# The last value chunk loaded into two spare half buffers in a two-part decode attention kernel

## The chip, the cores and the metric

The kernel runs on one core of one Trainium2 chip. The metric is the time on the device in microseconds (us), median of several executions. The record gives each execution a state; it was "fast" for every one (mean granted clock 0.93 to 0.94). Times in the traces count from the start of the span, which is 1.7 to 2.0 us shorter than the timed run.

## The reference

Two attention layers decode one token each for 4 sequences. A has 8 KV heads for 32 query heads and looks at the last 2048 keys; B has 32 heads of its own and looks at all 8192. Everything is bf16. The code is shortened.

```python
def _B_ref(x, k_cache, v_cache, wq, wo):          # A: the same on k_cache[:, :, Sk - W:, :], each KV head for 4 heads
    q = (x @ wq).reshape(B, Sq, H, Dh).transpose(0, 2, 1, 3)
    scores = jnp.einsum("bhqd,bhkd->bhqk", q, k_cache) * (Dh ** -0.5)
    p = _softmax(scores, axis=-1)
    o = jnp.einsum("bhqk,bhkd->bhqd", p, v_cache)
    return o.transpose(0, 2, 1, 3).reshape(B, Sq, H * Dh) @ wo
```

Only the caches are large: B's K and V are 268 MB each. The kernel has to stream them once.

## The kernel before

The work is cut into 72 chunks: 8 for A (c = 0 to 7, one KV head each) and 64 for B (c = 8 to 71, two heads of one sequence each, 4 MB of keys and 4 MB of values). K and V chunks go through ten half buffers of 16 KB per partition. B uses halves 0 to 3 for keys and 4 to 7 for values, two halves per chunk, in turn. Halves 8 and 9 serve A only.

```python
HALF_A = {"k": (2, 3, 8, 0, 1), "v": (6, 7, 9, 4, 5)}
LASTV = (64, 32, 16, 16)                           # the last value chunk comes in four pieces

def take(load, at, n, release):                    # a load waits for whatever last held its halves
    waits = []
    for i in range(at, at + n):
        waits += held[i]
        held[i] = [release]
    half_of[load] = at
    return waits

def dma_kv(kind, c):
    ...
    at = HALF_A[kind][c % 5] if ch["ab"] == 0 else (0 if kind == "k" else 4) + 2 * (c % 2)
    waits = take((kind, c), at, 1 if ch["ab"] == 0 else 2, ("T", ch["s_last"]) if kind == "k" else ("pv", c))
    ...
    if kind == "v" and c == NC - 1:
        j0 = 0
        for i, n in enumerate(LASTV):
            x = slice(j0 * P, (j0 + n) * P)
            sch.add_dma("sp", lambda e, x=x: e.dma_start(dst[:, x], src[:, x]), "d_vl%d" % i, waits=waits, key=("vl", j0))
            j0 += n
        return
    sch.add_dma("sp", lambda e: e.dma_start(dst, src), "d_h%d" % at, waits=waits, key=(kind, c))

loads = [("k", c + 1) for c in range(NC - 1)]      # each value chunk behind the next key chunk,
for c in range(NC):                                # but the last three at the very end
    loads.insert(2 * c + 1 if c < NC - 3 else len(loads), ("v", c))
```

(Cuts are marked with "...".) So the queue ends with k69, v68, k70, k71, v69, v70, v71. All loads go in this order through one queue. TensorE transposes a key chunk (T), makes scores (S), and multiplies weights with values (PV, 128 matmuls per chunk, "pv69" for chunk 69). In the loop the PV of one chunk is woven into the end of the next chunk's scores. At the end the order differs:

```python
for c in range(NC):
    keys_part(c)
    ...
    if c == NC - 2:
        emit_qb(c + 1)                             # no PV here
    else:
        values_part(None if c == 0 else c - 1 if c < NC - 1 else c - 2, c)
    if c == NC - 1:
        values_only(c - 1, c)                      # pv70
emit_fin(NC - 3)
emit_wos(NC - 1)
norm_sum(NC - 1)
values_only(NC - 1, NC)                            # pv71
emit_fin(NC - 1)
```

TensorE's program is a loop over pairs of chunks; chunks 70 and 71 stand behind it as straight code of 906 matmuls, each with its weight load.

## Time and profile before

| | before |
|---|---|
| time, median of the three runs given at the start | 1390.22 us (1389.66 to 1393.65) |
| span of the profiled run | 1388.5 us |
| bytes moved | 588 MB, mean 423 GB/s |
| TensorE / VectorE / ScalarE busy | 84% / 48% / 30% |
| waits of pv71 for its pieces of v71 | 5.16 us in all |

How to read it: "busy" of TensorE is an average over a kernel that waits for key chunks (150 us for B's, before the transposes), so it does not name the bound. The prediction shows the lines from which the bound is read. In these lines "tr" is T, "sc" is S, "po" is PV, "fin" is the output projection and "ms" a small sum; "issue" marks idle time in which the engine waited for nothing that the profile shows.

### The profile page before, as it was taken

How to read it: one execution, taken by the hardware profiler on the slowest of the kernel's cores; microseconds unless marked ns; L12 is line 12 of the kernel's file. 1: busy time of each engine (PE TensorE's matmuls, PEld its weight loads, DVE VectorE, ACT ScalarE, POOL GpSimd, SP SyncE). 2: the span in 40 equal slices, each digit the busy share in tenths (PEclk: the TensorE clock that was granted, in tenths of full speed). 3: DMA queues.
4: the chain of work that ended last, by engine and by line, in shares of the span. 5: the costliest groups of instructions: out<-in, count | busy, mean ns of one | idle time of the engine just before them, and what ended most of it. 6: DMA issues, size and time to landing. Idle time of an engine off the chain costs nothing.

```text
span 1388.5 us, 57015 instructions
## 1 busy us (share of the span) xinstructions
PE 1167.4 (84%) x26768; PEld 1124.6 (81%) x26768; DVE 673.0 (48%) x1327; ACT 422.9 (30%) x617; POOL 19.2 (1%) x22
## 2 busy tenths in 40 slices
PE   4778868998888888888888888988898888988887
PEld 4767868988888888888888888888888788887886
DVE  2877534554445444444445444544444444544452
ACT  1333322332233332332333232332233233332331
POOL 1111000000000000000000000000000000000000
PEclk9999989999999999999999999999999999999998
DMA  9999999999999999999999999999999999999995
GB/s 398 417 415 424 426 429 423 432 425 436 430 432 433 428 433 428 434 427 432 430 436 429 429 429 435 432 429 430 430 432 430 430 430 435 427 428 431 434 417 237
DMA packets 29992, 588.02 MB, mean 423 GB/s; under 512 B 2656, under 2 KB 10864, under 8 KB 11120
## 3 DMA queue, kind: packets, MB, share of 16 engines
q1 hardware_dynamic: 29912, 587.22, 99.0%
q8 instruction: 40, 0.66, 0.2%
q14 instruction: 16, 0.13, 0.0%
q10 hardware_dynamic: 24, 0.01, 0.0%
HBM read 587.21 MB, written 0.01 MB: 423 GB/s over the span
## 4 chain that ended last, share of the span: by engine, by line
DMA 60%; PE 33%; DVE 5%; issue 2%; ACT 0%; SPq 0%; DVEq 0%
DMA kv<-in_B_k_cache_dram 57%; PE tr L320 21%; PE sc L322 9%; DMA kv<-in_A_k_cache_dram 2%; PE po L322 2%; DVE kt L383 1%; DVE sA L432 1%; DMA kv<-in_B_v_cache_dram 1%; DVE rsa L500 1%; PE ms L322 1%; DVE sel L425 1%; DVE rm L442 0%; DVE sA L489 0%; DVE rs L498 0%; ACT eA L492 0%
## 5 line engine op out<-in xcount | busy, mean ns | idle before, releaser
L320 PE MATMUL tr<-identb,kv 128*128 128x128 bf16 x8704 | 699.7, 231 | 161.2 <-DMA kv<-in_B_k_cache_dram 150.2
L383 DVE COPY kt<-tr 128x1024 bf16<-128x1024 bf16 x736 | 502.8, 691 | 472.6 <-PE tr L320 468.6
L320 PEld LDWEIGHTS tr<-identb,kv 128*128 128x128 bf16 x8704 | 555.3, 104 | 187.6 <-issue 104.1
L381 ACT ACTIVATE kt<-tr 128x1024 bf16<-128x1024 bf16 x352 | 360.2, 1023 | 648.3 <-PE tr L320 645.7
L322 PE MATMUL sc<-qb,kt 128*128 128x64 bf16 x8192 | 422.4, 196 | 5.1 <-issue 2.9
L322 PEld LDWEIGHTS sc<-qb,kt 128*128 128x128 bf16 x8192 | 348.9, 100 | 8.7 <-issue 4.6
L322 PE MATMUL po<-pbb,kv 128*128 128x64 bf16 (+1 forms) x8192 | 290.8, 192 | 16.3 <-issue 10.9
L322 PEld LDWEIGHTS po<-pbb,kv 128*128 128x128 bf16 x8192 | 263.8, 97 | 15.8 <-issue 8.2
L481 ACT ACTIVATE pbb<-sc,negb 64x128 bf16<-64x128 f32 x128 | 51.1, 399 | 294.6 <-DVE negb L471 288.7
L447 DVE TENSOR_REDUCE rm<-sc 64x1 f32<-64x128 f32 x128 | 36.9, 289 | 94.0 <-PE sc L322 93.1
L322 PE MATMUL sc<-qs,kt 128*128 128x64 bf16 (+3 forms) x512 | 25.6, 194 | 17.0 <-DVE kt L383 17.0
L471 DVE COPY negb<-ms 128x1 f32<-128x1 f32 (+1 forms) x72 | 11.4, 158 | 52.6 <-PE ms L322 52.6
L322 PEld LDWEIGHTS sc<-qs,kt 128*128 128x128 bf16 x512 | 20.5, 99 | 20.1 <-DVE kt L383 20.0
L459 DVE TENSOR_REDUCE gm<-ms 1x2 f32<-1x128 f32 (+1 forms) x72 | 20.1, 279 | 31.3 <-PE ms L320 31.1
L322 PE MATMUL ms<-identf,gx 1*128 1x1 f32 (+1 forms) x144 | 27.2, 256 | 0.6 <-DVE gx L463 0.6
L322 PEld LDWEIGHTS ms<-identf,gx 1*128 1x128 f32 (+1 forms) x144 | 21.1, 182 | 4.9 <-DVE gx L463 0.8
L481 ACT ACTIVATION_READ_ACCUMULATOR pbb<-sc,negb 64x1 f32 x128 | 23.7, 185 | 0.0
L320 PE MATMUL ms<-identf,rm 128*1 128x128 f32 (+1 forms) x72 | 19.6, 273 | 0.2 <-DVE rm L447 0.2
L322 PE MATMUL fin<-wos,oz 128*4 128x512 bf16 x64 | 19.4, 385 | 0.3 <-DVE oz L541 0.3
L322 PE MATMUL po<-pba,kv 128*128 128x64 bf16 x512 | 18.8, 193 | 0.0
L432 DVE TENSOR_REDUCE sA<-sel 128x128 f32<-128x512 f32 x16 | 17.0, 1060 | 0.5
L463 DVE TENSOR_SCALAR gx<-gm 1x128 f32<-1x128 f32 (+1 forms) x72 | 16.0, 222 | 2.5
(46 smaller groups left out, 180.0 us busy)
## 6 DMA issues: line engine op xcount, KB each, us to landing
kv<-in_B_k_cache_dram SPq DMA_DIRECT2D x64, 4096.0 KB, 27.0
kv<-in_B_v_cache_dram SPq DMA_DIRECT2D x63, 4096.0 KB, 31.3
kv<-in_A_k_cache_dram SPq DMA_DIRECT2D x8, 2048.0 KB, 27.8
kv<-in_A_v_cache_dram SPq DMA_DIRECT2D x8, 2048.0 KB, 26.5
kv<-in_A_wq_dram SPq DMA_DIRECT2D x1, 4096.0 KB, 12.5
kv<-in_B_wq_dram SPq DMA_DIRECT2D x1, 4096.0 KB, 27.5
wor<-in_A_wo_dram SPq DMA_DIRECT2D x8, 512.0 KB, 23.4
wor<-in_B_wo_dram SPq DMA_DIRECT2D x8, 512.0 KB, 33.6
```

Source lines behind the costliest of these rows:

```text
L320: emit = lambda e: e.transpose(o, l, r)
L322: emit = lambda e: e.matmul(o, l, r, start=start, stop=stop)
L381: sch.add("act", lambda e: e.activation(dst, src, ACTF.Copy), waits=waits, key=("ev", s))
L383: sch.add("dve", lambda e: e.tensor_copy(dst, src), waits=waits, key=("ev", s))
L425: sch.add("dve", lambda e: e.tensor_tensor(out=sel[:, :].rearrange("p (j b c) -> p j b c", b=NB, c=REP), in0=sc[:, half, :].rearrange("p ( ...
L432: sch.add("dve", lambda e: e.tensor_reduce(out=dst, in_=sel[:, :].rearrange("p (j b c) -> p j c b", b=NB, c=REP), axis=AX.X, op=ALU.add), ...
L447: sch.add("dve", lambda e, src=src, pp=pp: e.tensor_reduce(out=rm[pp, m, 0:1], in_=src, axis=AX.X, op=ALU.max), waits=[("S", ch["s_last"]) ...
L459: sch.add("dve", lambda e: e.tensor_reduce(out=gm[0:C, m, 0:U], in_=src, axis=AX.X, op=ALU.max), waits=[("trm", c)], key=("gmax", c))
L463: sch.add("dve", lambda e: e.tensor_scalar(out=dst, in0=gv, scalar1=-scale, scalar2=None, op0=ALU.mult), waits=[("gmax", c)], key=("gx", c))
L471: sch.add("dve", lambda e: e.tensor_copy(negb[:, m, 0:C], ms[:, col:col + C]), waits=[("bc", c)], key=("negb", c))
L481: sch.add("act", lambda e, src=src, pp=pp, n=n, u=u: e.activation(pbv[pp, :, u], src, ACTF.Exp, bias=negb[pp, m, 0:1], scale=scale, accum_ ...
L500: sch.add("dve", lambda e: e.tensor_tensor(out=rst[0][:, m, :].rearrange("p (b c) -> p b c", b=NB), in0=bcast(rs4[:, m, :], [[0, NB], [1, ...
```

## The change

V71 has to wait for half 6 until pv69 is done, and pv69 comes late in the reordered tail. Halves 8 and 9 have been idle since chunk 7. The change puts v71 there:

```diff
             at = HALF_A[kind][c % 5] if ch["ab"] == 0 else (0 if kind == "k" else 4) + 2 * (c % 2)
+            if kind == "v" and c == NC - 1:
+                at = 8
             waits = take((kind, c), at, 1 if ch["ab"] == 0 else 2, ("T", ch["s_last"]) if kind == "k" else ("pv", c))
```

The intent is to issue v71 right behind v70, so that the stream has no hole and pv71 finds its data.

## The prediction

> **What bounds the kernel now.** I read the views from the coarse to the fine: the page, the waits of the DMA queue, the chain that ended last in its last 160 us, then the last 50 us engine by engine. The page first: the rows of the DMA busy share and of the bytes moved, in 40 slices of 34.7 us.
>
> ```profile
> DMA  9999999999999999999999999999999999999995
> GB/s 398 417 415 424 426 429 423 432 425 436 430 432 433 428 433 428 434 427 432 430 436 429 429 429 435 432 429 430 430 432 430 430 430 435 427 428 431 434 417 237
> q8 instruction: 40, 0.66, 0.2%
> ```
>
> The reader is to see a kernel that streams 588 MB at some 430 GB/s with no hole, except in the last slice: share 0.5, 237 GB/s. Nothing before the last slice can be gained by a change that moves no fewer bytes. What is left is the last 35 us. The third line counts fetches of instructions: 40 packets of 16 KB. It matters below.
>
> The waits of the DMA queue, and that queue's issues in order of time (start, duration, line):
>
> ```profile
> SPq L287 <- PE po L322: 34.5, 1, 34.5
> ...
> 1331.09 4.93 SPq L290 DMA_DIRECT2D kv<-in_B_v_cache_dram  x2
> 1370.51 1.85 SPq L287 DMA_DIRECT2D kv<-in_B_v_cache_dram  x4
> ```
>
> Line 287 is the load of the last value chunk, v71 (4 MB in four pieces). The two value chunks before it, v69 and v70, are issued at 1331.09 and 1335.69. Then the queue waits 34.5 us, once, for a PV group (out = weights times values) on TensorE. That is pv69: v71 goes to half 6, which v69 fills until pv69 ends at 1370.5. By the landings in the trace k71, v69 and v70 arrive at 1348.7, 1358.4 and 1368.1, so that the queue has run dry before v71 is issued. Busy time in stretches (length; PE, PEld, DVE, ACT, POOL; clock, DMA share, GB/s):
>
> ```profile
> 1356.00:1362.00 6.00, 4.25 (x91) 4.05 (x88) 2.82 (x7) 2.49 (x5) 0.00 (x0) 1.00 0.92 390
> 1362.00:1368.00 6.00, 5.77 (x162) 5.65 (x160) 2.82 (x6) 2.40 (x4) 0.00 (x0) 1.00 0.27 109
> 1368.00:1371.50 3.50, 3.24 (x96) 3.04 (x93) 1.06 (x5) 0.91 (x4) 0.00 (x0) 1.00 0.07 19
> 1371.50:1377.00 5.50, 4.00 (x113) 3.42 (x108) 0.52 (x2) 0.00 (x0) 0.00 (x0) 1.00 0.96 372
> ```
>
> The hole is from 1362 to 1371.5, and not sharp at its start: the completion packets of v70 lie between 1361.3 and 1367.6, so some of the 16 engines run 6 us behind others. The tail on TensorE (idle before, and its releaser, in brackets):
>
> ```profile
> 1358.51 0.29 PE L322 MATMUL sc<-qb,kt 128*128 128x64 bf16 x4 [1.75 <-issue]
> 1364.71 0.35 PE L322 MATMUL sc<-qb,kt 128*128 128x64 bf16 x6 [0.23 <-issue]
> 1370.74 3.92 PE L322 MATMUL po<-pbb,kv 128*128 128x64 bf16 x128 [0.26 <-DVE oz L541]
> 1374.59 0.59 PE L322 MATMUL fin<-wos,oz 128*4 128x512 bf16 x2
> 1375.11 0.39 PE L322 MATMUL ms<-rsb,onesf 128*128 128x4 f32 x2
> 1379.12 1.84 PE L322 MATMUL po<-pbb,kv 128*128 128x2 bf16 x64 [3.62 <-DMA kv<-in_B_v_cache_dram]
> 1381.64 1.01 PE L322 MATMUL po<-pbb,kv 128*128 128x2 bf16 x32 [0.67 <-DMA kv<-in_B_v_cache_dram]
> 1382.90 0.59 PE L322 MATMUL po<-pbb,kv 128*128 128x2 bf16 x16 [0.25 <-DMA kv<-in_B_v_cache_dram]
> 1384.11 0.58 PE L322 MATMUL po<-pbb,kv 128*128 128x2 bf16 x16 [0.62 <-DMA kv<-in_B_v_cache_dram]
> 1385.02 1.01 PE L322 MATMUL fin<-wos,oz 128*4 128x512 bf16 x2 [0.33 <-DVE oz L541]
> ```
>
> PV of chunk 70 is done at 1374.66, a last projection and a sum at 1375.5, and then TensorE waits 3.62 + 0.67 + 0.25 + 0.62 = 5.16 us for the pieces of v71. This wait is the whole of what the change can take away. After pv71 (1384.69) come 3.8 us that stay: normalisation, projection, copy, store, to 1388.5.
>
> [...] the landings 9.7 us apart agree with a stream in order. [...]the 40 packets are of 16,384 bytes; the two "issue" waits above lie exactly 256 TensorE instructions apart, the weight loads counted[...].
>
> **The change, part by part.**
>
> 1. Removed: the wait of v71 for pv69. Halves 8 and 9 were last used by key chunk 7 and value chunk 7 of the sliding part, done by about 130 us, so the new wait is over 1200 us before it is asked. v71 is issued right behind v70, at about 1336 to 1338 instead of 1370.5 to 1371.8. No instruction, byte or semaphore is added.
>
> 2. When v71 lands: the slowest engine ends v70 at 1367.6 and then has 256 KB of v71. It took 1.22 us per 32 KB: 9.8 us, so 1377.4, and about 0.5 us to the landing as with v70 (1367.6 to 1368.1): 1377.9 instead of 1384.1. The pieces: half at 1373.0, then 1375.4, 1376.7, 1377.9.
>
> 3. When TensorE could use it, if nothing else changed: from 1375.5. 128 matmuls with 2 columns, 64 in 1.84 us: 3.7 us, to 1379.2. The last 16 need the piece of 1377.9 and are reached at 1378.7, so the data is just in time. 1384.69 - 1379.2 = **5.5 us** gained at most.
>
> 4. What takes part of it back: the fetches. In the hole of before the DMA engines were free. Packet by packet: the block begun at 1358.51 has the fetch of its successor started at 1362.24, 3.7 us later; the one begun at 1364.71, in the hole, after 1.0 us; the one begun at about 1368.7 after 0.5 us; the one begun at 1373.2, with v71 flowing, after 3.4 us. From the start of a fetch to the first instruction of its block took 2.34 us (1356.17 to 1358.51) and 2.47 us (1362.24 to 1364.71) where TensorE stood waiting. So with the stream running a block of 256 can't come oftener than every 6.0 to 6.5 us, while the PV stretches use it in about 4. The straight code before the loop shows the same, again 256 instructions apart:
>
> ```profile
> 171.21 0.34 PE L322 MATMUL po<-pbb,kv 128*128 128x64 bf16 x6 [1.13 <-issue]
> 177.41 0.19 PE L322 MATMUL po<-pbb,kv 128*128 128x64 bf16 x1 [1.85 <-issue]
> ```
>
> With the change the stream has no hole. The block begun at 1364.71 is followed at 1364.71 + 6.2 to 6.5 = 1370.9 to 1371.2; TensorE gets there at 1368.7: 2.3 us lost. The next block begins near 1371.0 and TensorE is through it 4.5 us later, 1375.5; its successor arrives 2.9 us (an engine that has finished v71, as seven of them have by 1371.5) to 6.3 us (one still busy) after 1371.0, so 0 to 1.8 us are lost, 0.8 us as my middle. The one after that is asked for when most engines are free; nothing lost. Sum **3.1 us**.
>
> 5. So pv70 ends at 1374.66 + 3.1 = 1377.8, pv71 runs from 1378.6 to 1382.3, all of its data being there, and the end is 1384.69 - 1382.3 = **2.4 us** earlier.
>
> **Rivals.**
> (a) The fetches are quick enough: 5.5 us, 1384.7 us. For it: [...] the fetch in the hole may have been needed no sooner. Against: the 1.75 us at 1356.76 and the two lines above.
> (b) v71 is the new bound: a slow engine that also carries a fetch (each packet took about 1.1 us) ends v71 near 1378.5 to 1379.0, so pv71 ends at about 1379.7: 5.0 us gained if fetches don't stall TensorE, no change to point 5 if they do.
> (c) Both fetches fall on the engines that lag and stall 2.5 and 1.8 us, and a third stalls too: 5 us lost, gain near 0.5 us, 1389.7 us.
> (d) v71 in the queue early slows k71, v69 or v70: would cost up to 10 us. [...] I give it little.
> (e) It is hidden anyway: no, the 5.16 us of waits are on the chain that ended last.
>
> **Range and chances.** The timed median is 1390.22; point 5 gives 1390.2 - 2.4 = **1387.8 us**. Rival (a) at 1384.7 sets the lower side and (c) the upper; with the spread of the three runs of before (1389.66 to 1393.65) I take **1384.8 to 1390.2** for 8 in 10. 2% are 27.8 us, more than the whole stretch from the landing of v70 (1368.1) to the end of the span (20.4 us), so within 2% has **0.985**; faster 0.005, slower 0.01 for something unseen.
>
> **What the trace of after would show.** The four issues of v71 at 1336 to 1338 and no wait of 34 us on the queue; the DMA share over 0.9 from 1362 to about 1371, then falling; landings of v71 ending near 1378; no wait of the last PV for v_cache, or under 0.5 us; new "issue" waits of TensorE of 2 to 2.5 us in pv69 near 1369 and of 0 to 1.8 us in pv70 near 1375. Wrong it would be if these waits are missing (then it is faster, a), if they are longer or three (c), or if the landing of v71 slips beyond 1380.

5.5 us at most, less 3.1 us for the fetches, is the 2.4 us. A "block" in point 4 is 256 instructions of TensorE: that far apart lie the two "issue" waits that end at 1358.51 and 1364.71. Its 2.9 and 6.3 us for a fetch, and its 6.0 to 6.5 us for a block, are estimates from the times shown there: 0.5 us in the hole or 3.7 us in the stream until the fetch begins, and 2.34 to 2.47 us from there, which makes 2.8 to 6.2. That nothing can be gained before the last slice is an inference from the page (the load queue's packets fill 99.0% of the 16 engines' span; the full slices, the fourth to the 38th, carry 423 to 436 GB/s); no run tried a faster stream.

## The result

| | before | after |
|---|---|---|
| median, same rounds (4 runs each) | 1391.12 us | 1386.97 us (1385.85 to 1389.73) |
| span of the profiled run | 1388.5 us | 1384.0 us |
| v71 issued, from the span's start | 1370.5 to 1371.8 | 1339.6 to 1341.0 |
| v71 landed, last piece | 1384.06 | 1379.35 |
| pv71 | 1379.12 to 1384.69 | 1376.87 to 1380.22 |

The ratio is 0.9971 (95% interval 0.9949 to 0.9994): the mean time of one kernel's fast runs over that of the other's fast runs of the same rounds, so not quite the ratio of the medians above. It is 4.0 us, within 2%, but clear of zero. The predicted 1387.8 us lies 0.8 us from the measured median.

The page of the profile after, the same two rows of 40 slices:

```profile
DMA  9999999999999999999999999999999999999997
GB/s 398 416 416 423 425 428 421 417 428 434 430 433 430 428 431 434 429 428 432 430 434 430 429 431 433 431 427 432 429 435 429 431 430 433 431 429 430 430 409 319
```

The last slice has 319 GB/s instead of 237. What is missing to 430 now lies at its end (305 GB/s from 1371.5 to 1377, 20 from there to the last byte at 1379.35, no load after it), no longer in a hole within.

The issues of the DMA queue after (line numbers are two higher than before):

```profile
1334.60 4.93 SPq L292 DMA_DIRECT2D kv<-in_B_v_cache_dram  x2
1339.57 1.94 SPq L289 DMA_DIRECT2D kv<-in_B_v_cache_dram  x4
```

V71 follows v70 at once; the wait of 34.5 us is gone. Busy time in the stretches that the prediction shows of before:

```profile
1356.00:1362.00 6.00, 6.00 (x139) 5.92 (x136) 3.96 (x10) 3.97 (x7) 0.00 (x0) 1.00 1.01 434
1362.00:1368.00 6.00, 4.78 (x144) 4.55 (x139) 2.41 (x6) 1.02 (x1) 0.00 (x0) 1.00 0.95 404
1368.00:1371.50 3.50, 2.48 (x52) 2.26 (x53) 0.33 (x2) 0.70 (x3) 0.00 (x0) 0.80 0.94 400
1371.50:1377.00 5.50, 5.49 (x132) 4.90 (x130) 0.27 (x1) 0.21 (x2) 0.00 (x0) 0.82 0.75 305
```

The DMA share in the second and third stretch is 0.95 and 0.94, where it was 0.27 and 0.07. TensorE (first busy column) is less busy there than it was (4.78 against 5.77 us in 6; 2.48 against 3.24 in 3.5). Its timeline says why:

```profile
1366.58 0.19 PE L324 MATMUL po<-pbb,kv 128*128 128x64 bf16 x1
1368.76 1.08 PE L324 MATMUL po<-pbb,kv 128*128 128x64 bf16 x31 [1.98 <-issue]
...
1370.95 5.22 PE L324 MATMUL po<-pbb,kv 128*128 128x64 bf16 x128 [0.26 <-DVE oz L543]
1376.10 0.59 PE L324 MATMUL fin<-wos,oz 128*4 128x512 bf16 x2
1376.62 0.39 PE L324 MATMUL ms<-rsb,onesf 128*128 128x4 f32 x2
1376.87 3.35 PE L324 MATMUL po<-pbb,kv 128*128 128x2 bf16 x128
```

Three things are to be seen. Pv71 is one line of 128 matmuls and waits for nothing: the 5.16 us are gone. In pv69 TensorE stands still for 1.98 us and waits for nothing that the profile shows ("issue"). And pv70 takes 5.22 us where it took 3.92.

The trace's DMA packets settle the first of the two losses. The 256-instruction block whose first instruction comes at 1368.76 was fetched by a packet that began at 1366.25 and took 0.92 us; the block before it had begun at 1362.56. So the fetch began 3.7 us after that block, with the stream flowing, and its code ran 6.2 us after it.

The second loss has two parts. The next block boundary, at 1374.78, costs 0.20 us. The granted clock is at half from 1370.1 to 1373.5, and the starts of pv70's matmuls are 53 ns apart until 1373.45, then about 29: some 48 matmuls at 24 ns more, 1.1 us. The half clock began 1.3 us after the idle time of 1.98 us had ended and lasted 3.4 us.

### The profile page after: what moved, and what is told of

The parts are those of the page before. It is cut to its first block, busy times and chain, and to the rows that moved or that the text cites. A ratio compares the mean times of both kernels' runs of the same rounds, so it can differ in the third digit from the quotient of the medians.

```text
span 1384.0 us, 57015 instructions
## 1 busy us (share of the span) xinstructions
PE 1168.8 (84%) x26768; PEld 1125.1 (81%) x26768; DVE 672.5 (49%) x1327; ACT 422.9 (31%) x617; POOL 19.2 (1%) x22
## 4 chain that ended last, share of the span: by engine, by line
DMA 58%; PE 35%; DVE 5%; issue 2%; ACT 0%; SPq 0%; DVEq 0%
DMA kv<-in_B_k_cache_dram 55%; PE tr L322 21%; PE sc L324 9%; PE po L324 3%; DMA kv<-in_A_k_cache_dram 2%; DVE kt L385 1%; DVE sA L434 1%; DVE rsa L502 1%; PE ms L324 1%; DVE sel L427 1%; DVE rm L444 0%; DVE sA L491 0%; DVE rs L500 0%; ACT eA L494 0%; PE fin L324 0%
```

## The experiments

All kernels are edits of the changed one unless said. Calls of four runs shared the runs of the kernel before, whose medians were 1391.13, 1390.85 and 1389.52 us. The second of these calls (before_again, after_third, small16, small32) ran on another chip than the other two, so ratios are compared, not times.

**The changed kernel again, three times (after_again, after_third, after_fourth).** No edit.

> The changed kernel unaltered, for a tighter time and a second profile. Theory (the wait for v71 is gone, TensorE is the bound of the tail and stalls for instruction blocks while the stream runs): 3.5 to 5 us under the kernel before, ratio about 0.997; a stall of about 2 us in pv69, 256 instructions before a second, smaller one in pv70; no wait of pv71 for the value load. Rival (the first profile was a lucky one and the gain is the 2.4 us of the prediction): ratio 0.998 and a second stall of about 1 us.

> The changed kernel unaltered, on the same chip as the two with small rows: ratio 0.997, a stall of 2 us in pv69, no wait of pv71 for the load.

> The changed kernel unaltered, beside the two in plain order, and one more sample of the scatter between loads of one program (0.9972 and 0.9979 so far): ratio 0.9965 to 0.9985; a stall of about 2 us in pv69, the first stall (of the first block after chunk 70) anywhere from 0 to 2.2 us.

Measured: 1386.45, 1388.78 and 1387.18 us; ratios 0.9972 (0.9957 to 0.9987), 0.9979 (0.9965 to 0.9993), 0.9985 (0.9972 to 0.9999). Pv71 waits for no load in any of them. The stalls (times that TensorE waits for "issue") differ: 0.51 and 1.98 us in the first, 2.02 and 2.24 in the second, 2.02, 1.06 and 0.41 in the third, so the second stall in pv70 that I expected came in after_fourth alone. This is after_third, the one with most of them:

```profile
1357.59 0.29 PE L324 MATMUL sc<-qb,kt 128*128 128x64 bf16 x4 [2.02 <-issue]
1371.36 1.38 PE L324 MATMUL po<-pbb,kv 128*128 128x64 bf16 x31 [2.24 <-issue]
1374.05 6.04 PE L324 MATMUL po<-pbb,kv 128*128 128x64 bf16 x128 [0.26 <-DVE oz L543]
```

The half clock lay at 1358.3 for 3.4 us and at 1372.0 for 6.8 us, right behind both stalls, and pv70 took 6.04 us. The same program thus has a tail that varies by some 5 us.

**The kernel before as a kernel of its own, twice (before_again, before_third).** No edit of the kernel before.

> The kernel before, unaltered, for a second profile of its tail and for the noise: ratio 1.000 within 0.0015. Theory: waits of pv71 for its pieces of about 5 us together; the first stall for a block (1.75 us in the first profile, 0 in the late_wait profile, whose tail is the same code) comes out anywhere between 0 and 2 us, because it depends on how long the fetch stands behind the stream. Rival (that stall belongs to the kernel before): 1.75 us again.

> The kernel before, unaltered, a further sample of the scatter between loads (0.9984 when run as a kernel of its own): ratio 0.998 to 1.001; pv71 waits about 5 us for its pieces; fetches in the hole start about 1 us after their block, those under the stream 3 to 6 us.

Measured: 1388.53 us, ratio 0.9984 (0.9968 to 0.9999), and 1390.79 us, ratio 1.0006 (0.9992 to 1.002). The first misses my band of 0.0015: the same program, run in another place of the call, differed by 0.16%, so the intervals do not cover all of the scatter. Waits for v71's pieces were 5.21 and 5.17 us. Before_again had one stall, of 0.95 us; before_third had 0.35, 1.48 and 1.05. The 1.75 us of the first profile is therefore not a property of the kernel before.

**The old wait put back, the new place kept (late_wait).**

```diff
             waits = take(...)
+            if kind == "v" and c == NC - 1:
+                waits = waits + [("pv", c - 2)]
```

> v71 in the free halves, but with the old wait for pv69 put back. Theory (the gain is the wait alone): the time of the kernel before, ratio 0.999 to 1.001; the issue of v71 again near 1370, a hole in the stream, 5 us of waits of pv71 for its pieces. Rival (the place in memory matters, or the end of the wait on another buffer): the time of the changed kernel, ratio 0.997.

Measured: 1390.89 us, ratio 1.0 (0.9986 to 1.0014). The queue and the tail of TensorE:

```profile
1333.13 4.93 SPq L294 DMA_DIRECT2D kv<-in_B_v_cache_dram  x2
1370.24 1.85 SPq L291 DMA_DIRECT2D kv<-in_B_v_cache_dram  x4
```

```profile
1370.47 3.92 PE L326 MATMUL po<-pbb,kv 128*128 128x64 bf16 x128 [0.26 <-DVE oz L545]
1379.17 1.86 PE L326 MATMUL po<-pbb,kv 128*128 128x2 bf16 x64 [3.94 <-DMA kv<-in_B_v_cache_dram]
```

V71 is issued at 1370.24 again, and pv71 waits 3.94 us for its first piece (5.45 in all). The gain is the wait and nothing of the place.

**V71 loaded but not read (loaded_not_read; result wrong).** Pv71 multiplies with v69's half and waits for no load; the queue waits for the unused load at the very end.

```diff
+            if kind == "v" and c == NC - 1:
+                half_of[("v", c)] = half_of[("v", c - 2)]     # after take(...): the load itself still goes to halves 8, 9
...
-                    waits += [("vl", j)] if ("vl", j) in sch.tk else []
+                    pass
...
+            for i in range(len(LASTV)):
+                e.wait_ge(sems["d_vl%d" % i], 16)
```

> v71 loaded as in the changed kernel, but pv71 multiplies with v69's half and waits for no load (a wrong result on purpose). Theory (TensorE's own work and its blocks of instructions are the bound): the time of the changed kernel within 0.5 us, the same stalls. Rival (the landing of the last piece of v71, 1379.35, is the bound): up to 1 us faster than the changed kernel.

Measured: 1387.85 us, ratio 0.9983 (0.9969 to 0.9997), that is 1.5 us more than after_again, with overlapping intervals. I had expected it within 0.5 us, the rival up to 1 us less. Stalls of 1.48 and 1.98 us:

```profile
1358.69 0.29 PE L326 MATMUL sc<-qb,kt 128*128 128x64 bf16 x4 [1.48 <-issue]
1370.81 1.08 PE L326 MATMUL po<-pbb,kv 128*128 128x64 bf16 x31 [1.98 <-issue]
1372.81 5.46 PE L326 MATMUL po<-pbb,kv 128*128 128x64 bf16 x128 [0.26 <-DVE oz L545]
```

Freeing pv71 of the load bought nothing, which speaks against the landing of v71 as the bound of the changed kernel; in its own profiles pv71 waits for no load either.

**V71 not loaded at all (not_loaded; result wrong).**

```diff
             if kind == "v" and c == NC - 1:
-                at = 8
+                half_of[("v", c)] = half_of[("v", c - 2)]
+                return
```

> v71 not loaded at all, pv71 multiplies with v69's half (a wrong result on purpose). Theory (the fetch of an instruction block waits behind the stream's packets): fetches after 1362 start 0.5 to 1 us after the block before begins, not 3.5 to 4; the 2 us stall in pv69 is gone or under 0.5 us; 2 to 3 us faster than the changed kernel, ratio to the kernel before 0.995. Rival (the stall in pv69 has nothing to do with the load of v71): the stall and the time as in the changed kernel, 0.997.

Measured: 1385.55 us, ratio 0.9961 (0.9947 to 0.9975): 1.5 us under after_again, where I had expected 2 to 3, and 3.1 us under loaded_not_read by the ratios.

```profile
1359.77 0.32 PE L325 MATMUL sc<-qb,kt 128*128 128x64 bf16 x4 [2.02 <-issue]
1373.20 3.92 PE L325 MATMUL po<-pbb,kv 128*128 128x64 bf16 x128 [0.26 <-DVE oz L544]
```

The stall of 2.02 us while v70 still streams is there; the one in pv69 is gone, and pv70 is back to 3.92 us. The last four fetches that the tail needed began 0.1 to 0.4 us after the block before them, with no stream in the way. The pair of loaded_not_read and not_loaded differs in the load alone, which nobody reads. The intervals of the two times just overlap; it is the traces, one of each, with the late fetch and its stall in the one and neither in the other, that show the load's traffic to cost TensorE time through the fetches.

**Smaller rows in the last loads (small16, small32).** K71, v69, v70 and v71 in pieces of 16 or 32 tiles, so 4 or 8 KB per partition instead of 32. The edit for 32 (for 16: eight pieces):

```diff
-LASTV = (64, 32, 16, 16)
+LASTV = (32,) * 4
+SMALL = 32
...
+            if (kind, c) in (("k", NC - 1), ("v", NC - 3), ("v", NC - 2)):
+                for j0 in range(0, NTB, SMALL):
+                    x = slice(j0 * P, (j0 + SMALL) * P)
+                    sch.add_dma("sp", lambda e, x=x: e.dma_start(dst[:, x], src[:, x]), "d_h%d" % at, waits=waits,
+                                key=(kind, c) if j0 == NTB - SMALL else None)
+                return
```

> The changed kernel with k71, v69, v70 and v71 loaded in 8 pieces each of 4 KB per partition, instead of 32 KB. Theory (an instruction fetch stands behind a number of packets of the stream, so it waits a time proportional to their size): fetches after 1345 start under 1 us after the block before begins instead of 3.5 to 6, no stall over 0.3 us in pv69 and pv70; TensorE is then early, pv71 waits for its last pieces, end 0.5 to 1.5 us before the changed kernel's, less what the small packets slow the stream (0.16 us per 4 KB against 1.22 per 32 KB: up to 5% of 39 us). Rival (the fetch waits a fixed time or number of bytes): fetches 3.5 us or more late, the 2 us stall in pv69 stays, time as the changed kernel's or 1 to 2 us more.

> The same with 4 pieces of 8 KB per partition, a size at which the stream of the first profile lost nothing (0.305 us per packet). Theory: fetches start 1 to 1.5 us after the block before begins, stalls under 0.5 us, end 0.5 to 1.5 us before the changed kernel's, ratio to the kernel before 0.9965. Rival: as the changed kernel, stall of 2 us, 0.997.

Measured: 1387.10 us, ratio 0.9968 (0.9955 to 0.9982), and 1385.69 us, ratio 0.9961 (0.9947 to 0.9974). The idea of the mechanism fell: behind rows of 4 KB the fetches still began 2.1 to 3.6 us after the block before them, behind 8 KB 2.9 to 3.6 (1.1 as the stream ended). Small16:

```profile
1368.53 1.08 PE L331 MATMUL po<-pbb,kv 128*128 128x64 bf16 x31 [1.54 <-issue]
1371.37 2.68 PE L331 MATMUL po<-pbb,kv 128*128 128x64 bf16 x86 [1.10 <-DMA kv<-in_B_v_cache_dram]
1374.55 1.39 PE L331 MATMUL po<-pbb,kv 128*128 128x64 bf16 x42 [0.51 <-issue]
```

With 4 KB rows the stream got slower: from the landing of k70 to the last landing 40.5 us against 39.0 in every profile of the changed kernel, and pv70 and pv71 waited 1.1 us each for data. Small32 took 39.6. Small32 was 2.5 us under after_third by the ratios, with overlapping intervals; neither profile had one of the long first stalls. Whether that is the small rows or chance I can't say.

**The plain order at the end (plain_free, plain_old).** All value chunks follow the next key chunk, as in the loop, and the PV of the last chunks is woven in as in the loop. TensorE's loop then takes one more turn; 131 matmuls are left behind it instead of 906. Plain_free has v71 in halves 8 and 9, plain_old in half 6.

```diff
-            loads.insert(2 * c + 1 if c < NC - 3 else len(loads), ("v", c))
+            loads.insert(2 * c + 1, ("v", c))
...
-            if c == NC - 2:
-                emit_qb(c + 1)
-            else:
-                values_part(None if c == 0 else c - 1 if c < NC - 1 else c - 2, c)
-            if c == NC - 1:
-                values_only(c - 1, c)
-        emit_fin(NC - 3)
+            values_part(None if c == 0 else c - 1, c)
+        sch.mark()
```

The rest of the edit drops the special cases of the last chunk in keys_part, and adds one harmless copy so that the last turn has the counts of the others.

> v71 in the free halves, and the last two key chunks in the plain order of the loop (each value chunk loaded right after the next key chunk; PV interleaved as in the loop), so that TensorE's loop takes one more turn and only 131 matmuls are left behind it instead of 906. Theory (blocks of instructions fetched behind the stream hold TensorE up in the tail): no instruction fetch and no issue stall between 1340 and 1371; k71 lands 9.7 us later (near 1358.5), its 12 us of transposes and scores, 5 us of PV and pv71 end near 1380, the span near 1384: as the best profile of the changed kernel (1384.0), 0 to 3.5 us better than its others; ratio to the kernel before 0.996 to 0.997. Rival (the stalls cost nothing on the whole, and the early k71 is worth its 9.7 us): slower than the changed kernel, ratio 0.999 or more.

> The same plain order with v71 in the old half 6. There pv69 is over near 1357, before v70 has landed, so the old wait should leave no hole in the stream. Theory (the free halves help only because the old order puts pv69 late): same time as plain_free within 0.001, v71 issued near 1357, no wait of pv71 over 1 us. Rival (free halves help by themselves): 3 us more than plain_free.

Measured: 1385.94 us, ratio 0.9976 (0.9962 to 0.999), and 1386.36 us, ratio 0.998 (0.9967 to 0.9994). After_fourth had 0.9985. In plain_old:

```profile
1358.66 1.51 PE L320 MATMUL tr<-identb,kv 128*128 128x128 bf16 x24 [2.21 <-DMA kv<-in_B_k_cache_dram]
1375.55 0.39 PE L322 MATMUL ms<-rsb,onesf 128*128 128x4 f32 x2 [0.86 <-ACT pbb L482]
1379.55 1.01 PE L322 MATMUL fin<-wos,oz 128*4 128x512 bf16 x2 [0.33 <-DVE oz L542]
```

These are all the waits of TensorE after 1340 in that profile: none for "issue". There is one instruction fetch between 1300 us and the end, at 1378.6. V71 is issued at 1356.5, with v70 still on its way until 1368.3, so the old half does no harm. The two kernels are the same within the scatter, as expected: the free halves help only because the reordered tail puts pv69 late. The hoped-for 0 to 3.5 us over the changed kernel came out as 0.7 to 1.3 us with overlapping intervals; k71 lands 9.7 us later, which I take to eat up much of what the stalls cost; no run separates the two.

## Why the prediction was right or wrong

The profiles together (stalls are TensorE's "issue" waits after the landing of k70; the last column is the end of the span minus that landing, which takes out what happened before the tail):

| profile | pv71 waits for v71 | stalls | k70 landed to end |
|---|---|---|---|
| before | 5.16 | 1.75 + 0.23 | 49.5 |
| before_again | 5.21 | 0.95 | 47.1 |
| before_third | 5.17 | 0.35 + 1.48 + 1.05 | 50.6 |
| late_wait | 5.45 | 0 | 47.5 |
| after | 0 | 1.98 | 43.6 |
| after_again | 0 | 0.51 + 1.98 | 45.4 |
| after_third | 0 | 2.02 + 2.24 | 48.5 |
| after_fourth | 0 | 2.02 + 1.06 + 0.41 | 46.4 |

The mean of the last column is 48.7 us in the first four and 46.0 in the last four: 2.7 us. The four ratios of the changed kernel have a mean of 0.9977, 3.2 us; the kernel before run as its own and late_wait have 0.9997. So the gain is about 3 us, between the 2.4 us of the prediction and the 4.0 us of the first measurement, and the scatter of one program between runs and calls is as large as half of it.

- **Point 1, the wait removed:** right. V71 was issued right behind v70, and late_wait, with the wait put back, has the time and the 5.45 us of waits of the kernel before.
- **Point 2, the landing:** right. V71's last piece came 9.81 us after v70 in the first profile; 9.8 were worked out.
- **Point 3, at most 5.5 us:** the wait is gone whole. Pv71 itself took 3.35 us, not 3.7. (The 5.5 us are more than the 5.16 us that the prediction calls "the whole", since pv71 in four pieces also ran a little longer.)
- **Point 4, the fetches take part of it back:** the mechanism is right, by not_loaded against loaded_not_read and by the straight code's absence in plain_free and plain_old. The stall in pv69 was put at 2.3 us and measured 1.98, 1.98, 2.24 and 1.06. The stall in pv70, put at 0.8, measured 0.2, 0, 0 and 0.41.
- **The term that was mis-sized in point 4:** I took the first stall of the kernel before (1.75 us) as a fixed cost that both kernels share. It is chance: with the same code it came out between 0 and 2.02 us, since the fetch of that block began between 2.9 and 6.1 us after the block before it. In the first pair of profiles before had 1.98 us of stalls and after 1.98, so that nothing was taken back by them in this pair; over four profiles each the mean is 1.5 us before and 3.1 us after, so some 1.6 us are taken back where I had 3.1.
- **What the sum did not have:** the clock. In the tails above and in the experiments all seven stalls of 1.98 us or more were followed within 2.3 us by 3.4 or 6.8 us of half clock; none of the fourteen of 1.75 us or less was. In the kernel before the half clock fell into pv71's waiting, from 1375 to 1381 on, where it cost little (in the first profile pv71's matmuls took 4.0 us in all, with half clock from 1379.47; in after, at full clock, 3.35); in the changed kernel TensorE is the bound, and pv70 took 5.22, 5.97 and 6.04 us in the first three profiles of it, against 3.92. At 24 ns for each slow matmul that is 1.1, 2.1 and 2.1 us, and none in after_fourth: 1.3 us in the mean.
- **When a stall costs clock:** its length alone does not decide. Plain_old's wait of 2.21 us for k71, shown above, was followed by no half clock, and between 320 and 1348 us only 61 of 166 idle times of 1.98 to 2.24 us in the fourteen traces were. The clock record changes only at the ends of fixed steps of 3.41 us (in the traces of before and after each of its stretches but the last is a whole multiple of that), so I take of each idle time of 1 us or more (after 320 us, 733 in all) the longest part that lies inside one step. Where that part was 2.2 us or more, the half clock began during the idle time or within 2.5 us after it in 399 of 399 cases; from 1.8 to 2.2 us in 90 of 134; below 1.8 us in 1 of 200. In the traces of before and after alone it is 61 of 61, 12 of 18 and 0 of 25. So in these traces the half clock went with how much of a stall fell into one step. This is a count over traces; no experiment moved a stall on purpose.
- **Luck:** that 2.4 us came so near is in part luck. The stalls took back 1.5 us less than I had, and the clock, which I did not have, some 1.3 us in pv70 alone.
- **Loose readings in the prediction:** half 8 and 9 were free at 137 us, not 130; and a block "every 6.0 to 6.5 us" came out as 5.2 to 8.5 where TensorE stood waiting for it.
- **The rivals:** (a) did not hold, the stalls are there. (b) did not hold, loaded_not_read was not faster. (c) after_third comes near it in size, its tail being 48.5 us long against a mean of 48.7 before, but not in kind: it stalled before pv69 and in pv69, and in pv70 it lost to the clock. (d) did not show: k71, v69 and v70 landed 9.7 us apart as before. (e) did not hold.

What stays open is why a fetch waits between 2.4 and 6.1 us behind the stream in one and the same program, and why smaller rows don't shorten it. No kernel with a right result is shown to be faster than the changed one: small16, small32, plain_free and plain_old came out 0.7 to 2.5 us lower by their ratios than the changed kernel in the same call, inside the scatter.

## What to carry to other kernels

When a stream is the bound, look for a load at its end that waits for a buffer, and look for a buffer that an earlier stage left idle: here the move itself cost nothing (late_wait, the new place with the old wait: ratio 1.0). Ask then what else lived in the hole that you close; here it was the fetch of instructions, which TensorE's loop did without (none on its queue between 283.01 and 1347.39 us in after) and its straight code did not (seven from there to the end, of 0.9 to 1.4 us each). And when the gain is 0.2%, run the old kernel under its own name too, or the scatter between calls is taken for an effect.
